# Attention and two MoE layers in one core: a new written order, single dummy products, and gap clears of their own

## The chip, the cores and the metric

The kernel runs on one NeuronCore of a Trainium2 chip. The metric is device time in microseconds (us) from start to end of one execution. The engines are TensorE (PE: matrix products; PEld: its weight loads), VectorE (DVE), ScalarE (ACT), GpSimd (POOL) and SyncE (SP), whose queue issues nearly all DMAs.

## The reference

Windowed attention feeds two MoE layers, all in float32. Cut to what matters:

```python
def _attn_ref(q, k, v):                  # (2, 8, 768, 64)
    k_sum = k.reshape(B, H, nb, 32, D).max(axis=3)
    v_sum = v.reshape(B, H, nb, 32, D).mean(axis=3)
    # scores against keys within 16 positions, and against the 24 block maxima (+ log 32)
    a = softmax(concat(masked local scores, block scores))
    return a @ concat(v, v_sum)
x = attn_out as (1536 tokens, 512)
x = relu(x @ w_in1) ** 2 @ w_out1        # d_ff 2048
h = x @ w_in2
out = (P(h) / Q(h)) @ w_out2             # cubic P, quadratic Q
```

## The kernel before, in words

The attention works in 24 pieces `d`, each a quarter of the heads for 256 tokens; two pieces form a unit `u`, and two units a group of 256 tokens. The first MoE layer takes the tokens in three chunks of 512, in passes over slices `f` of 128 hidden columns; each pair (chunk, slice) is a step `g`. Products of the MoE layers are made in three parts (high times high, high times low, low times high) of 128x512, so every operand exists as a rounded high tile (`wh`, `xh`, `sh`) and the remainder (`wl`, `xl`, `sl`).

In the first stage the order is written out by hand: `ORDER` is a string of short names, each the name of a part and a number, and each engine gets its instructions in that order. A star makes DVE do the part where ACT (copies) or POOL would. Parts that matter here:

- `E`, `F`: the two key loads of head pair p (L305); `t`: 8 transposes of keys into two PSUM banks (L386, `pk`); `K`: clears the gaps beside the keys in those banks (L377), which `t` does itself unless `K` came earlier; `k`, `l`: copies into `kt` (L398); `c`, `B`: block maxima and their copies (L406, L412).
- `q`, `z`: query transposes and copy (L451, L458). `s`: scores (L473, `pss`). `m`, `e`, `r`, `n`: mask and maximum on DVE (L489), exponential on ACT (L498), sum and reciprocal on DVE (L506, L507), and the scaling `pr` (L513), on POOL, or DVE with a star. `p`, `b`: transposes (L523, `ptp`) and copy (L527). `o`, `x`, `y`: product with the values (L543, `pav`) and the high and low parts of the result (L560, L565).
- `V`: block sums of the values on PE (L425, `pvs`). `S`: sums of the values on POOL ahead of them (L330 for the first half, L338 with the tile `vst` for the second).
- `I`: weight load; `T`, `D`, `W`, `M`: decode on ACT (L140) and DVE (L148, L149), high part (L160), low part (L165, POOL, or DVE with a star).
- `h`: a quarter of a step's first product (L596); `i`, `j`: ReLU on ACT (L606) and square on DVE (L611); `G`, `H`: high and low part of it (L659, L666); `Y`: a quarter of the second product (L690).
- `X`: `keep_busy`, dummy products of zeros (L283) into the PSUM bank `h0`, which reads a part of the tile `pp0`.

In the first two chunks of the first pass all steps share the bank `h0`, so the first quarter of step g+1 (`h` 4g+4) waits for `j` g, which reads that bank last. There are seven PSUM banks for everything else of the attention; `bank` hands them out in the order in which they come free. SP issues its DMAs in order. After `ORDER` a loop (`main_loop`) issues all the rest by rules; the change does not touch it.

Of the kernel before, what the change touches and what calls it, by code (L numbers as in the profile page):

```python
# [16 lines left out]


ORDER = (
# [26 lines left out]
)  # L46


# [1 line left out]
def tile_window_attention_moe_moe(  # L50
# [13 lines left out]
    nc = tc.nc  # L64
# [3 lines left out]
    P = 128  # L68
# [107 lines left out]
    T6 = 6  # L176
    bt = ap.tile([P, WT + (T6 // 2 + 1) * NB], F32, name="b6", bufs=1)
    b6 = [bt[:, r * NB:r * NB + HK] for r in range(T6 // 2)]
# [94 lines left out]
    idle = pps[0][:, 0]  # L273
    spare = []
# [2 lines left out]
        nc.vector.memset(idle, 0.0)  # L277
        spare.append(ps_h.tile([P, 512], F32, tag="h0", name="spare"))

    def keep_busy(n):  # L280

        for _ in range(n):
            nc.tensor.matmul(spare[0][:, 0:P], lhsT=idle, rhs=idle, start=True, stop=True)  # L283

    consts = dict(
        _i0=c_idle,
        _id=lambda: make_identity(nc, ident), _pr=c_more,
        _m0=lambda: nc.vector.memset(wide, 0.0), _m1=c_window,
        _ml=lambda: nc.vector.memset(mk[:, :, WT:], math.log(BLK) * SC), _m2=c_masks, _b8=c_blocks, _bw=c_blocks6,
# [281 lines left out]
    N0 = [0, 5, NF, NF + 9]  # L571
# [167 lines left out]
    G1 = len(tok1) * FS[0] - LEAD[0]  # L739
    dve, act = nc.vector.tensor_copy, nc.scalar.copy  # L740
    some, rest = slice(0, 4), slice(4, NWIN)
    v0 = [early[4 + p][:, 0:2 * T6 * D].rearrange("p (h r d) -> p h r d", r=T6, d=D) for p in range(NP)]
# [5 lines left out]
    def w_next(j, *a):  # L748
# [16 lines left out]
        M=lambda k, c=None: w_low(*divmod(k, 2), vec(c)), O=lambda i: keep(("y0", "y1", "y2", "y3")),  # L765
        h=lambda i: l1(*divmod(i, 4)), i=elem_1, j=elem_2, G=elem_4, H=lambda g, c=None: elem_5(g, vec(c)),
        Y=lambda i: l2(*divmod(i, 4)), X=keep_busy, K=k_gap,
    )
    NW = 4 * NF
    G2 = len(tok1) * FS[0] + len(tok2) * FS[1]  # L770
# [122 lines left out]
```

## Time and profile before

| what | value |
|---|---|
| median of 3 runs | 615.32 us (614.94 to 616.34) |
| the profiled execution | 614.9 us, of it the span from first to last instruction 613.1 us |
| PE busy | 593.2 us, 97% of the span |
| DVE, ACT, POOL busy | 65%, 64%, 49% |
| mean granted TensorE clock | 0.994 |

Busy shares are means over stages with different limits: the written order fills roughly the first quarter of the span, and there the shares differ from the rest. A PE row with a count lists that many instructions from the start of the first to the end of the last; one dummy product counts as two. The PE clock column gives the share of 2.4 GHz that was granted; 0.50 is 1.2 GHz.

### The profile page before, as it was taken

The page shows a single profiled execution, that of the slowest core. Times are in us where ns is not written, and L with a number is a line of the kernel's source. Part 1 is how long each engine was busy: PE and PEld are TensorE (multiplying, and loading weights), DVE is VectorE, ACT ScalarE, POOL GpSimd, SP SyncE. Part 2 cuts the span into 40 slices and gives each one's busy share as a digit, 9 for nine tenths or more (in the row PEclk, how much of TensorE's full clock was granted, in tenths as well). Part 3 has the DMA queues.
Part 4 walks back from the last instruction along what each step waited for, and adds up shares of the span by engine and source line. Part 5 has one row for each costly group of instructions (what it writes and reads, how often), then busy time and mean ns, then how long its engine had stood idle before and what let it go on. Part 6 is the DMA issues. An engine that isn't in the chain of part 4 may idle for free.

```text
span 613.1 us, 9335 instructions
## 1 busy us (share of the span) xinstructions
PE 593.2 (97%) x3338; PEld 488.4 (80%) x3338; DVE 400.8 (65%) x828; ACT 391.3 (64%) x704; POOL 303.5 (49%) x289
## 2 busy tenths in 40 slices
PE   7778999999999999999999999999999999999997
PEld 7666777788888888888888888888888888888885
DVE  4999977977752232111357487898787876686765
ACT  2888866645654443222456589888888987777772
POOL 1355564220454445122567477757565664455442
PEclk9899989999999999999999999999999999999999
DMA  9979954454533330000045202212121200010101
GB/s 176 251 168 225 238 142 93 102 146 151 164 111 103 104 89 15 0 1 1 2 162 182 68 1 69 68 36 68 35 69 35 69 2 0 1 68 2 41 29 68
DMA packets 69981, 51.45 MB, mean 84 GB/s; under 512 B 46000, under 2 KB 63664, under 8 KB 69936
## 3 DMA queue, kind: packets, MB, share of 16 engines
q1 hardware_dynamic: 69792, 50.74, 30.7%
q8 instruction: 26, 0.43, 0.3%
q14 instruction: 19, 0.16, 0.1%
q10 hardware_dynamic: 144, 0.13, 0.1%
HBM read 47.71 MB, written 3.15 MB: 83 GB/s over the span
## 4 chain that ended last, share of the span: by engine, by line
PE 89%; DVE 8%; ACT 1%; DMA 1%; issue 1%; SPq 0%; DVEq 0%; ACTq 0%
PE h L596 42%; PE y L690 41%; PE ptp L523 2%; PE pav L543 1%; PE pss L473 1%; DVE pr L489 1%; PE pk L386 1%; DVE pr L513 1%; DVE wdec L149 1%; DVE mx L506 1%; DMA early<-in_k_dram 1%; DVE kss L406 1%; DVE xl L565 1%; DVE kt L412 0%; PE spare L283 0%
## 5 line engine op out<-in xcount | busy, mean ns | idle before, releaser
L596 PE MATMUL h<-xh,wh 128*128 128x512 f32 x384 | 151.3, 394 | 0.8 <-DVE r L611 0.8
L596 PE MATMUL h<-xl,wh 128*128 128x512 f32 x384 | 150.0, 391 | 0.0
L596 PE MATMUL h<-xh,wl 128*128 128x512 f32 x384 | 150.0, 391 | 0.0
L620 POOL TENSOR_TENSOR q<-q,u 128x512 f32<-128x512 f32 x48 | 64.6, 1346 | 95.7 <-ACT q L617 95.7
L611 DVE TENSOR_TENSOR r<-r,h 128x512 f32<-128x512 f32 x48 | 32.9, 686 | 113.6 <-ACT r L606 106.0
L165 POOL TENSOR_TENSOR wl<-wdec,wh 128x512 fp32r<-128x512 f32 x56 | 73.7, 1323 | 62.5 <-ACT wh L160 60.6
L666 POOL TENSOR_TENSOR sl<-r,sh 128x512 fp32r<-128x512 f32 x39 | 51.1, 1313 | 90.5 <-PE y L690 77.4
L596 PEld LDWEIGHTS h<-xh,wh 128*128 128x128 f32 x384 | 72.7, 189 | 15.7 <-DVE r L611 1.0
L596 PEld LDWEIGHTS h<-xh,wl 128*128 128x128 f32 x384 | 72.4, 188 | 15.3 <-DVE wl L165 0.3
L596 PEld LDWEIGHTS h<-xl,wh 128*128 128x128 f32 x384 | 72.5, 189 | 14.9
L690 PE MATMUL y<-sh,wh 128*128 128x512 f32 x192 | 75.5, 393 | 0.0
L690 PE MATMUL y<-wh,sl 128*128 128x512 f32 x192 | 74.9, 390 | 0.1
L690 PE MATMUL y<-sl,wh 128*128 128x512 f32 x192 | 74.8, 390 | 0.0
L690 PE MATMUL y<-wl,sh 128*128 128x512 f32 x192 | 74.7, 389 | 0.0
L690 PE MATMUL y<-wh,sh 128*128 128x512 f32 x192 | 74.7, 389 | 0.0
L690 PE MATMUL y<-sh,wl 128*128 128x512 f32 x192 | 74.7, 389 | 0.0
L606 ACT ACTIVATE r<-h 128x512 f32<-128x512 f32 x48 | 28.6, 595 | 71.7 <-PE h L596 36.7
L666 POOL TENSOR_TENSOR sl<-p,sh 128x512 fp32r<-128x512 f32 x48 | 63.6, 1326 | 9.0 <-ACT sh L659 7.3
L642 DVE SCALAR_TENSOR_TENSOR q<-q,h 128x512 f32<-128x512 f32 x48 | 32.9, 686 | 41.4 <-ACT h L638 40.2
L160 ACT CAST wh<-wdec 128x512 fp32r<-128x512 f32 x64 | 39.6, 620 | 26.2 <-DVE wdec L149 26.0
L149 DVE SCALAR_TENSOR_TENSOR wdec<-wraw,wdec 128x512 int32<-128x512 int32 x64 | 53.6, 838 | 2.2
L616 ACT ACTIVATE u<-h 128x512 f32<-128x512 f32 x48 | 28.5, 594 | 30.6 <-PE h L596 30.5
(92 smaller groups left out, 1030.5 us busy)
## 6 DMA issues: line engine op xcount, KB each, us to landing
wraw<-in_moe_w_in_dram SPq DMA_DIRECT2D x32, 512.0 KB, 3.8
wraw<-in_moe_w_out_dram SPq DMA_DIRECT2D x32, 512.0 KB, 3.3
early<-in_v_dram SPq DMA_DIRECT2D x40, 96.0 KB, 4.3
out_dram<-acc SPq DMA_DIRECT2D x11, 256.0 KB, 2.1
acc<-in_q_dram SPq DMA_DIRECT2D x10, 256.0 KB, 5.5
early<-in_k_dram SPq DMA_DIRECT2D x8, 192.0 KB, 4.6
kst<-in_k_dram SPq DMA_DIRECT2D x8, 192.0 KB, 6.5
early<-in_v_dram SPq DMA_DIRECT2D x4, 384.0 KB, 6.1
```

The costliest lines, as they stand in the source:

```text
L149: nc.vector.scalar_tensor_tensor(out=t, in0=low, scalar=29, in1=t, op0=ALU.logical_shift_right, op1=ALU.bitwise_or)
L160: copy(out=wt[n][0][:, j], in_=f32(wdec[n, j]))
L165: eng.tensor_tensor(out=tl[:, j], in0=t, in1=f32(th[:, j]), op=ALU.subtract)
L523: nc.tensor.transpose(out=pt[0:HK, c * P:(c + 1) * P], in_=pr[:, c, 0:HK], identity=ident)
L596: nc.tensor.matmul(hq[g][:, 0:n], lhsT=w[:, 0, ws], rhs=x[:, part, ts], start=(part == 0 and j == 0), stop=(part == KC - 1 and j == 2),)
L606: nc.scalar.activation(out=r, in_=hq[g][:, 0:n], func=AF.Relu)
L611: nc.vector.tensor_tensor(out=eq[g], in0=eq[g], in1=hq.pop(g)[:, 0:n], op=ALU.mult)
L616: nc.scalar.activation(out=u_, in_=hq[g][:, 0:n], func=AF.Abs)
L620: nc.gpsimd.tensor_tensor(out=q_, in0=q_, in1=u_, op=ALU.mult)
L642: nc.vector.scalar_tensor_tensor(out=q_, in0=q_, scalar=1.0 + 1e-6, in1=z_, op0=ALU.add, op1=ALU.mult)
L666: eng.tensor_tensor(out=sl[:, 0:n], in0=eq.pop(g), in1=f32(sh[:, 0:n]), op=ALU.subtract)
L690: nc.tensor.matmul(o, lhsT=lt, rhs=rt, start=(f == 0 and j == 0 and d * m % 512 == 0), stop=(f == FS[ps] - 1 and j == 2 and (d + 1) * m % ...
```

## The change

The string `ORDER` is replaced by another one, of 695 names instead of 655. `X` becomes a single dummy product and appears 36 times (before three times, with 8, 2 and 3 products). `K` appears for all eight head pairs, so that every clear is a part of its own. The set of other parts is the same, with stars on other ones: `n*` 10 to 5, `H*` 9 to 3, `M*` 8 to 10, `k*` 1 to 3, `l*` 3 to 1, `b*` 5 to 7, `z*` 3 to 2, `B*` 4 to 5, `u*` 0 to 1, `w*` 1 to 0. Of the dummy products, 31 numbers run in order and five (31 to 35) stand at the front.

```diff
-    "_b8 F0 _id _m0 _m1 E2 _i0 F2 X8 t2 X2 K0 E0 t0 l0 l2* F1 E1 t1 k0 _ml k2* c2 B2* q_0 _pr X3 "
-    "c0 B0* k1 l1 c1 F3 q0 z0 s0 _m2 s1 m1 e1 Q1 _bw E3 t3 l3 m0 r1 n1* q_1 q1 z1* k3 e0 r0 q2 "
-    "c3 B3 s2 s3 m2 n0 z2 B1 J1 e2 v1 p0 m3 e3 N0 b0 v0 p1 b1 r2 n2* S0 s4 s5 m4 q3 z3 p2 m5 r3 "
...
+    "K3 _i0 X31 E1 F0 _id X32 X33 X34 _m0 X35 X0 X1 _m1 _m2 E0 K1 _ml X2 F1 t1 k1 l1 K0 t0 E2 "
+    "k0* X3 X4 X5 q_0 F2 _b8 q0 X6 l0 X7 X8 K2 z0 t2 c0 s0 c1 k2* s1 B1* l2 c2 B2* X9 q_1 B0 q1 "
+    "X10 X11 X12 m0 e0 m1 _pr e1 r0 z1 E3 F3 t3 X13 X14 X15 X16 X17 X18 v0 S0 s2 k3 n0 p0 v1 Q1 "
...
         nc.vector.memset(idle, 0.0)
         spare.append(ps_h.tile([P, 512], F32, tag="h0", name="spare"))
 
-    def keep_busy(n):
-
-        for _ in range(n):
-            nc.tensor.matmul(spare[0][:, 0:P], lhsT=idle, rhs=idle, start=True, stop=True)
+    def keep_busy(i):
+
+        nc.tensor.matmul(spare[0][:, 0:P], lhsT=idle, rhs=idle, start=True, stop=True)
 
     consts = dict(
         _i0=c_idle,

```

The first place is the start of PE's queue. `spare` are the dummy products, `pk` the key transposes, `pt` the query transposes, `pss` the scores. Before:

```order
L283 MATMUL spare<-pp_87 128x128 x8
L386 MATMUL pk<-ident,early 128x96 x8
L283 MATMUL spare<-pp_87 128x128 x2
L386 MATMUL pk<-ident,early 128x96 x16
L283 MATMUL spare<-pp_87 128x128 x3
L451 MATMUL pt<-ident,acc 128x128 x4
L473 MATMUL pss<-kt_98,qz_85 64x120 x8
L473 MATMUL pss<-kt_99,qz_85 64x120 x8
L386 MATMUL pk<-ident,early 128x96 x8
L451 MATMUL pt<-ident,acc 128x128 x8
L473 MATMUL pss<-kt_100,qz_86 64x120 x8
```

and with the change:

```order
L284 MATMUL spare<-pp_87 128x128 x8
L387 MATMUL pk<-ident,early 128x96 x16
L284 MATMUL spare<-pp_87 128x128 x3
L452 MATMUL pt<-ident,acc 128x128 x4
L284 MATMUL spare<-pp_87 128x128 x3
L387 MATMUL pk<-ident,early 128x96 x8
L474 MATMUL pss<-kt_98,qz_85 64x120 x8
L474 MATMUL pss<-kt_99,qz_85 64x120 x8
L284 MATMUL spare<-pp_87 128x128
L452 MATMUL pt<-ident,acc 128x128 x4
L284 MATMUL spare<-pp_87 128x128 x3
L387 MATMUL pk<-ident,early 128x96 x8
```

Two key pairs are now transposed together ahead of the first query transposes, in place of one, and single dummy products stand in five places ahead of and around the first scores.

The second place is DVE's queue ahead of the first square (`r`, of step 0, L611 before and L612 now), which frees the bank for the second step. `kss` are block maxima, `mx`, `rs` sums and reciprocals, `wdec` decoded weights. Before:

```order
L406 TENSOR_REDUCE kss_94<-kt_98 128x24
L412 COPY kt_98<-kss_94 128x4x24
L506 TENSOR_REDUCE mx_91<-pr_104 128x4
L507 RECIPROCAL rs_93<-mx_91 128x4
L565 TENSOR_TENSOR xl<-pav,xh 128x2x256
L148 TENSOR_SCALAR wdec<-wdec 128x512
L149 SCALAR_TENSOR_TENSOR wdec<-wraw,wdec 128x512
L458 COPY qz_85<-pt 128x512
L377 MEMSET pk 128x5x4 x2
L148 TENSOR_SCALAR wdec<-wdec 128x512
L149 SCALAR_TENSOR_TENSOR wdec<-wraw,wdec 128x512
L611 TENSOR_TENSOR r<-r,h 128x512
```

and with the change:

```order
L507 TENSOR_REDUCE mx_90<-pr_103 128x4
L508 RECIPROCAL rs_92<-mx_90 128x4
L566 TENSOR_TENSOR xl<-pav,xh 128x2x256
L150 TENSOR_SCALAR wdec<-wdec 128x512
L151 SCALAR_TENSOR_TENSOR wdec<-wraw,wdec 128x512
L407 TENSOR_REDUCE kss_95<-kt_99 128x24
L413 COPY kt_99<-kss_95 128x4x24
L378 MEMSET pk 128x5x4 x2
L612 TENSOR_TENSOR r<-r,h 128x512
```

Before, two weight tiles, a query copy and one more block maximum stand between the last value part and the square; with the change one weight tile and one block maximum do. Over the whole queue ahead of this square the counts go from 4 to 3 decoded tiles, 7 to 6 block maxima, 12 to 11 sums and reciprocals, 16 to 12 scalings (instructions), 2 to 1 copies of `pp` and of `qz`, 3 to 4 copies L398 and 9 to 8 copies L412. On PE, ahead of the first product of the second step, they go from 64 to 56 key transposes, 120 to 112 score products, and 13 to 36 dummy products.

The third place is POOL's queue around the first sums of the values of the second half (`vst`). Before:

```order
L513 TENSOR_SCALAR pr_102<-pr_102,rs_92 128x120 x4
L666 TENSOR_TENSOR sl<-r,sh 128x512
L338 TENSOR_TENSOR vst<-vst 96x2x256 x2
L338 TENSOR_TENSOR vst<-vst 96x2x128 x2
L338 TENSOR_TENSOR vst<-vst 96x2x64 x2
L513 TENSOR_SCALAR pr_102<-pr_102,rs_93 128x120 x4
L165 TENSOR_TENSOR wl<-wdec,wh 128x512 x2
L513 TENSOR_SCALAR pr_103<-pr_103,rs_92 128x120 x4
L338 TENSOR_TENSOR vst<-vst 96x2x256 x2
```

and with the change:

```order
L514 TENSOR_SCALAR pr_102<-pr_102,rs_92 128x120 x4
L339 TENSOR_TENSOR vst<-vst 96x2x256 x2
L339 TENSOR_TENSOR vst<-vst 96x2x128 x2
L339 TENSOR_TENSOR vst<-vst 96x2x64 x2
L514 TENSOR_SCALAR pr_103<-pr_103,rs_93 128x120 x4
L167 TENSOR_TENSOR wl<-wdec,wh 128x512
L514 TENSOR_SCALAR pr_104<-pr_104,rs_92 128x120 x4
L667 TENSOR_TENSOR sl<-r,sh 128x512
L514 TENSOR_SCALAR pr_102<-pr_102,rs_93 128x120 x4
L167 TENSOR_TENSOR wl<-wdec,wh 128x512
L339 TENSOR_TENSOR vst<-vst 96x2x256 x2
```

Between the two rounds of sums POOL now has three sets of scalings and one `sl`, where it had two sets; over the whole program POOL's scalings go from 56 to 76 instructions, its `sl` from 87 to 93 and its `wl` from 56 to 54.

## Rows read from the trace of the kernel before

**Rows 1.** The page: its first line, the span.
```profile
span 613.1 us, 9335 instructions
```

**Rows 2.** Windows: stretch, then us PE, PEld, DVE, ACT, POOL busy (count), clock, DMA, GB/s.
```profile
0.00:57.57 57.57, 45.25 (x570) 38.10 (x570) 46.72 (x203) 39.25 (x98) 20.12 (x49) 0.97 0.96 199
57.57:118.00 60.43, 57.18 (x549) 44.95 (x549) 51.33 (x173) 41.88 (x103) 33.23 (x49) 0.97 0.68 163
118.00:250.00 132.00, 131.97 (x640) 109.01 (x640) 65.81 (x115) 63.73 (x113) 52.59 (x43) 1.00 0.33 103
...
30.00:57.57 27.57, 22.12 (x339) 17.80 (x338) 26.82 (x99) 23.25 (x58) 14.06 (x28) 1.00 0.84 184
```

**Rows 3.** Timeline of PE, first 58 us: start, us, engine, line, operation, idle before.
```profile
1.25 3.78 PE L283 MATMUL spare<-pp 120*128 120x128 f32 x16 [1.25 <-DVE pp L277]
6.63 1.52 PE L386 MATMUL pk<-ident,early 96*128 96x96 f32 x8 [1.60 <-DMA early<-in_k_dram]
...
16.56 1.51 PE L386 MATMUL pk<-ident,early 96*128 96x96 f32 x8 [1.34 <-DVE pk L377]
...
33.98 0.85 PE L386 MATMUL pk<-ident,kst 96*128 96x96 f32 x8 [0.95 <-issue]
34.76 0.64 PE L473 MATMUL pss<-kt,qz 64*64 64x120 f32 x16
...
57.57 0.50 PE L596 MATMUL h<-xh,wh 128*128 128x512 f32 x1 [0.80 <-DVE r L611]
```

**Rows 4.** Windows (columns as rows 2) where the clock falls and rises.
```profile
16.50:17.00 0.50, 0.44 (x3) 0.47 (x4) 0.50 (x7) 0.37 (x2) 0.36 (x2) 0.50 1.06 310
19.50:20.00 0.50, 0.50 (x10) 0.29 (x12) 0.23 (x2) 0.40 (x2) 0.00 (x0) 0.61 0.85 264
78.00:81.00 3.00, 3.00 (x8) 2.34 (x9) 2.97 (x18) 2.46 (x6) 0.69 (x3) 0.50 0.00 0
```

**Rows 5.** Timelines of SP and DVE, first 12 us.
```profile
0.80 4.38 SPq L305 DMA_DIRECT2D early<-in_k_dram  x6
...
7.54 0.76 DVE L398 COPY kt<-pk 128x576 f32<-128x576 f32 x1 [6.21 <-PE pk L386]
```

**Rows 6.** DVE by line, 0 to 57.57 us: count | busy, mean ns | idle before.
```profile
L506 DVE TENSOR_REDUCE mx<-pr 128x4 f32<-128x484 f32 x12 | 7.8, 647 | 0.3 <-ACT pr L498 0.3
...
L406 DVE TENSOR_REDUCE kss<-kt 128x24 f32<-128x768 f32 x7 | 6.6, 942 | 0.9 <-ACT kt L398 0.9
...
L149 DVE SCALAR_TENSOR_TENSOR wdec<-wraw,wdec 128x512 int32<-128x512 int32 x4 | 3.8, 940 | 0.1
...
L398 DVE COPY kt<-pk 128x576 f32<-128x576 f32 x3 | 2.3, 754 | 6.2 <-PE pk L386 6.2
...
L148 DVE TENSOR_SCALAR wdec<-wdec 128x512 int32<-128x512 int32 x4 | 1.7, 413 | 0.0
...
L458 DVE COPY qz<-pt 128x512 f32<-128x512 f32 x2 | 1.4, 688 | 0.0
```

**Rows 7.** PE waits, 57 to 140 us: who waited for whom, us, times, longest.
```profile
PE ptp L523 <- DVE pr L513: 3.1, 5, 1.2
```

**Rows 8.** Timelines of DVE and POOL, 18 to 80 us.
```profile
18.09 0.86 DVE L513 TENSOR_SCALAR pr<-pr,rs 128x120 f32<-128x120 f32 x4
...
53.47 0.69 DVE L149 SCALAR_TENSOR_TENSOR wdec<-wraw,wdec 128x512 int32<-128x512 int32 x1
...
55.28 1.64 DVE L149 SCALAR_TENSOR_TENSOR wdec<-wraw,wdec 128x512 int32<-128x512 int32 x1
...
74.88 3.05 DVE L513 TENSOR_SCALAR pr<-pr,rs 128x120 f32<-128x120 f32 x4
...
55.08 1.29 POOL L165 TENSOR_TENSOR wl<-wdec,wh 128x512 fp32r<-128x512 f32 x1 [3.48 <-ACT wh L160]
...
72.67 5.58 POOL L338 TENSOR_TENSOR vst<-vst 96x512 f32<-96x512 f32 x6
```

**Rows 9.** POOL by line, 0 to 250 us.
```profile
L513 POOL TENSOR_SCALAR pr<-pr,rs 128x120 f32<-128x120 f32 x56 | 22.0, 413 | 22.7 <-DVE rs L507 9.3 <-DVE pr L513 5.1 <-DVE mx L489 5.0
```

48 rows, old and new, of the table ORDER are left out of this document.

## The prediction

> **What bounds the kernel now.** I read the busy time by stretches first, to find where TensorE (PE) is not at work, then PE's timeline and waits in those stretches, then the engine it waits for. The span is 613.1 us [rows 1] and the profiled execution 614.9, so 1.8 lies around it; the median of the runs, 615.32, is 0.4 above that execution.
>
> The stretches show three stages. To 57.57 us PE is busy 45.25 of 57.57; to 118 it is busy 57.18 of 60.43; from 118 on it hardly stops (131.97 of 132) [rows 2]. The change touches the written order only, and what follows it is PE work without gaps, so whatever PE gains or loses ahead of 118 us moves the end by the same amount.
>
> In the first stage PE is not the limit. From 30 to 57.57 us VectorE (DVE) is busy 26.82 of 27.57, PE 22.12 [rows 2]. The stage ends where PE gets the first product of the second step, at 57.57, released by the square (L611) on DVE [rows 3]. So here DVE's queue sets the pace, and PE's empty 12.3 us are the price.
>
> In the second stage PE loses 3.25 us [rows 2], 3.1 of it in five waits of the transposes `ptp` for scalings made on DVE [rows 7]. One row shows how: a set of four scalings that takes 0.86 us takes 3.05 at 74.88, while POOL runs its value sums from 72.67 for 5.58 [rows 8]. Behind that wait the granted clock is 0.50 from 78 to 81 us [rows 4]: 3.0 us that do the work of 1.5. The second stage thus gives away 3.25 + 1.5 = 4.75 us.
>
> **The change, part by part.** *Start.* SP issues six key loads in 4.38 us, 0.73 each [rows 5]. Before, the first transposes needed the third load and began at 6.63 [rows 3]; now they need the fourth: 0.7 later. Ahead of the first scores stand the same three sets of key transposes, and 14 dummy products in place of 13; the eight at the front fall in the wait for the keys. A dummy product is two rows: 3.78 / 16 x 2 = 0.47 us [rows 3]. That clock is the half one, although the column shows 1.00 up to its first fall: eight key transposes take 1.52 at 6.63, as at 16.56 (1.51, clock 0.50), but 0.85 at 33.98 [rows 3, 4]. At full clock a dummy product would thus take 0.47 x 0.85 / 1.52 = 0.26. The start costs between nothing (DVE, idle until 7.54 [rows 5], has further gaps to catch up in: 57.57 - 46.72 = 10.85 idle [rows 2], so 3.3 behind 7.54) and 0.73 + 0.47 = 1.2. I take **+0.7**, since both ends are near.
>
> *DVE ahead of the first square.* By the counts of the two orders DVE has there one decoded weight tile less (L148 0.41 + L149 0.69), one block maximum (0.94), one sum (0.65), one set of scalings (0.86), and two copies from PSUM (0.69 each), but one key copy more (0.75) [rows 6, 8]: 1.10 + 0.94 + 0.65 + 0.86 + 1.38 - 0.75 = 4.2. As DVE is busy 97% there, all of it is on the path: **-4.2**.
>
> *What is late next.* The 23 added dummy products are PE work: 23 x 0.26 = 6.0 us at full clock, 10.8 at half. They stand in PE's in-order queue ahead of real work. PE's 12.3 empty us take them in sum, but not each in its place. ScalarE, busy 23.25 of 27.57 in the same stretch [rows 2], becomes as loaded as DVE once that has 4.2 less. The waits that come of both lie between 0 and 4.2 (all of DVE's gain). I take **+1.5**, nearer to the low end, because after the dummies PE still has 1.5 to 6.3 us free.
>
> *Work put behind.* Ahead of the second step's first product PE now has eight key transposes and eight score products less. From the starts of the two rows the transposes take 34.76 - 33.98 = 0.78; eight score products are 16 rows, 0.64 [rows 3]. That work is done later, when PE has no gaps: **+1.4**.
>
> *Clears.* The clears of the key gaps keep their number over the program; two of them are moved across the first square. They cost nothing as long as each is early; a late one shows as a wait of `pk` for L377, as the 1.34 at 16.56 [rows 3], and it would cost at most that.
>
> *Second stage.* Of the ten starred scaling sets five stay on DVE, and only two of those come behind the first square. The two kinds of PE wait named above should go, with the fall of the clock behind one of them. In their place a scaling takes 4 x 0.41 = 1.65 us on POOL [rows 9] instead of 0.86, behind whatever POOL holds. Of the 4.75 us lost between nothing and all stays. I take 2.0, about the two waits' share if POOL's extra 0.8 shows two or three times: **-2.75**.
>
> Against it stands DVE beside POOL: L149 takes 1.64 at 55.28, where a POOL subtraction began at 55.08 for 1.29, and 0.69 at 53.47 [rows 8]. The Trainium skill (SBUF — State Buffer, section "SBUF: two separate sides") states that the two engines share a port pair as an exclusive lock, held for the whole instruction by whichever starts first, so that the other blocks. By that rule POOL's 24 added instructions could each hold DVE; ten holds of 0.95 would turn the sum below into a loss of 6 us. I add nothing for it, because the 20 scalings and 6 subtractions that leave DVE are themselves instructions that could be held.
>
> *Sum:* 0.7 - 4.2 + 1.5 + 1.4 - 2.75 = -3.35. The profiled execution would be 614.9 - 3.35 = 611.55, the median 0.4 more: **612.0**. With every bound at its good end, 0 - 4.2 + 0 + 1.4 - 4.75 = -7.55 (607.8); at its bad end, 1.2 - 4.2 + 4.2 + 1.4 + 0 = +2.6 (617.9).
>
> **The rivals.** *All fed.* The order fits: no new waits on the ramp and no PE wait in the second stage. 607.8. For it: DVE, ScalarE and POOL all have free time between 57.57 and 118 [rows 2]. Against: with much the same free time PE waited five times there before [rows 7].
>
> *Nothing won on the ramp.* The dummy products or ScalarE stand where DVE stood, and the second step starts where it did: 0.7 - 4.2 + 4.2 + 1.4 - 2.75 = -0.65, that is 614.7. For it: ScalarE's 23.25 of 27.57.
>
> *The clock is not held.* Dummy products may not bring the full clock earlier, as the eight at the front did not before. Then 23 x 0.21 = 4.8 us more PE work stands in the queue; about half would meet empty time, +2.4, so 614.4. The trace speaks against it: the clock rises at 19.5 to 20.0 us [rows 4] behind the key transposes of 16.56 [rows 3] and the query transposes that follow them in the order, with no dummy product there. The Trainium skill (TensorE: Matmul & The Clock Gate, section "Part 4: PE-mode transpose") says instead that transposes do not count as PE work for the full clock. That rise disagrees with the rule, so this case gets little.
>
> *Slower: POOL becomes the bound.* A scaling that now follows a round of value sums on POOL waits up to 5.58 us [rows 8]; there are two such rounds. If PE has some 2 us of other work until the transposes need it, each costs 3.6, together 7.2, and with one fall of the clock (1.5) 8.7 in place of 4.75. With the ramp's -0.6 that is +3.35, so 618.7. It decides from some 5.4 us lost in the second stage on, that is, when both rounds hit and not one. Against it: the same sums stand ahead of scalings now, and PE's waits there are for DVE's.
>
> **How the numbers follow.** Chances: forecast 0.45, all fed 0.20, nothing won on the ramp 0.17, POOL as bound 0.12, clock not held 0.06. A measurement here tells 0.2%, 1.2 us, from no change. Faster than 614.1: 0.43 of the forecast, all of the second, 0.06 of the third and 0.03 of the last, 0.72. Slower than 616.5: most of POOL's case and 0.03 of the third, 0.14. The rest, 0.14, is no change. The range leaves out POOL's case and takes in the second to half a microsecond beyond it: 607.3 to 616.5. The forecast's own range is 610 to 614.
>
> **What would show it.** Right: the first product of the second step starts near 57.57 + 0.7 - 4.2 + 1.5 = 55.6 us; PE's waits for DVE's scalings are gone between there and 118 us; the clock stays at 1.00 from some 14 us on; no set of DVE scalings takes 3 us before the stage's end. Wrong: that product at 57 us or later (then the ramp term failed, and the wait ahead of it names what took DVE's place), or `ptp` waiting for POOL's scalings by more than 2 us in sum, or a stretch at clock 0.50 behind 20 us.

## The result, and the profile after

The changed kernel takes 605.31 us (median of 4 runs, 603.71 to 605.96) against 615.13 on the same chip; the ratio is 0.9833, 95% interval 0.9809 to 0.9856. A second measurement, on the chip of the last two experiments, gave 605.56 against 614.71: 0.9853 (0.9834 to 0.9871). The forecast was 612.0 with a range of 607.3 to 616.5. The sign was right; the gain is 9 to 10 us where 3.3 was forecast, and the time lies under the range. The profiled execution took 605.37 us.

The page's first line and its row of TensorE's clock, after:

```profile
span 603.6 us, 9425 instructions
...
PEclk9999999999999999999999999999999999999999
```

The windows of the changed kernel, with the columns of [rows 2]: the three stages, cut at the second step's first product, and then the short stretches of [rows 4].

```profile
0.00:52.75 52.75, 45.86 (x592) 40.46 (x593) 40.52 (x196) 36.93 (x95) 22.23 (x53) 1.00 1.00 213
52.75:118.00 65.25, 64.02 (x647) 52.22 (x646) 53.10 (x177) 46.62 (x112) 42.61 (x67) 1.00 0.73 158
118.00:250.00 132.00, 132.00 (x611) 109.11 (x609) 60.95 (x96) 61.94 (x107) 59.17 (x45) 1.00 0.32 102
16.50:17.00 0.50, 0.50 (x9) 0.50 (x7) 0.50 (x7) 0.50 (x2) 0.50 (x1) 1.00 1.28 214
19.50:20.00 0.50, 0.50 (x17) 0.34 (x17) 0.50 (x1) 0.36 (x1) 0.50 (x2) 1.00 1.08 383
78.00:81.00 3.00, 3.00 (x42) 2.23 (x41) 2.40 (x4) 3.00 (x10) 0.42 (x2) 1.00 1.15 225
```

PE is without work for 6.9 us of the first stage and 1.2 us of the second, where before it was 12.3 and 3.25, and the clock does not fall. (As before, the column's 1.00 hides the half clock of the start: 16 key transposes take 2.79 us at 7.59, eight take 0.83 at 13.15. Three of the eight executions of the change have a mean clock of 0.996 to 0.998 and took 603.71, 605.29 and 607.21 us, so a fall somewhere need not show in the time.) Its timeline, first 53 us (columns of [rows 3]):

```profile
1.23 3.78 PE L284 MATMUL spare<-pp 120*128 120x128 f32 x16 [1.23 <-DVE pp L279]
7.59 2.79 PE L387 MATMUL pk<-ident,early 96*128 96x96 f32 x16 [2.58 <-DMA early<-in_k_dram]
...
13.15 0.83 PE L387 MATMUL pk<-ident,early 96*128 96x96 f32 x8
...
16.32 0.83 PE L387 MATMUL pk<-ident,early 96*128 96x96 f32 x8
16.98 1.53 PE L284 MATMUL spare<-pp 120*128 120x128 f32 x12
19.38 0.64 PE L474 MATMUL pss<-kt,qz 64*64 64x120 f32 x16 [0.87 <-ACT qz L459]
...
52.75 0.48 PE L597 MATMUL h<-xh,wh 128*128 128x512 f32 x1
```

The second step's first product, the thirteenth `h`, starts at 52.75 (53.12 in the second measurement's trace) instead of 57.57 [rows 3], and no longer waits for the square. The key transposes at 13.15 and 16.32 take 0.83 us, where those at 16.56 took 1.51 [rows 3]. Six dummy products (12 rows, 1.53 us) stand in the wait for the query copy, of which 0.87 us are left. All waits of PE over the whole program:

```profile
PE pk L387 <- DMA early<-in_k_dram: 2.6, 1, 2.6
PE pav L544 <- ACT pp L528: 1.7, 2, 1.4
PE spare L284 <- DVE pp L279: 1.2, 1, 1.2
PE h L597 <- DVE wl L167: 1.1, 2, 0.6
PE pss L474 <- ACT qz L459: 0.9, 1, 0.9
PE pav L544 <- DVE pp L528: 0.3, 1, 0.3
```

The five waits for DVE's scalings [rows 7] are gone. Scalings now stand on POOL 76 times (before 56, [rows 9]), hardly slower each (POOL by line, 0 to 250 us):

```profile
L514 POOL TENSOR_SCALAR pr<-pr,rs 128x120 f32<-128x120 f32 x76 | 30.6, 421 | 20.0 <-DVE rs L508 12.9 <-DVE mx L490 3.1 <-PE y L691 2.3
```

So of the span's 9.5 us, 4.8 are won ahead of the thirteenth product and 4.7 behind it (9.3 = 4.45 + 4.85 in the second measurement). The forecast had 2.0 and 1.35.

### The profile page after: what moved, and what is told of

Its sections match the earlier page's. It is cut to its first block, busy times and chain, and to the rows that moved or that the text cites. A ratio compares the mean times of both kernels' runs of the same rounds, so it can differ in the third digit from the quotient of the medians.

```text
span 603.6 us, 9425 instructions
## 1 busy us (share of the span) xinstructions
PE 591.5 (98%) x3384; PEld 490.5 (81%) x3384; DVE 389.3 (64%) x806; ACT 390.0 (65%) x702; POOL 319.6 (53%) x313
## 4 chain that ended last, share of the span: by engine, by line
PE 91%; ACT 4%; DVE 2%; DMA 2%; issue 0%; SPq 0%; DVEq 0%; ACTq 0%
PE h L597 43%; PE y L691 41%; PE pav L544 2%; ACT pr L499 2%; PE ptp L524 1%; PE pss L474 1%; PE pk L387 1%; DMA wraw<-in_moe_w_in_dram 1%; DMA early<-in_k_dram 1%; PE pt L452 1%; ACT pp L528 0%; PE pvs L426 0%; PE spare L284 0%; DVE acc L723 0%; SPq L306 0%
## 5 line engine op out<-in xcount | busy, mean ns | idle before, releaser
L667 POOL TENSOR_TENSOR sl<-r,sh 128x512 fp32r<-128x512 f32 x45 | 60.3, 1342 | 105.5 <-PE y L691 78.8
L612 DVE TENSOR_TENSOR r<-r,h 128x512 f32<-128x512 f32 x48 | 32.9, 685 | 108.8 <-ACT r L607 101.2
L167 POOL TENSOR_TENSOR wl<-wdec,wh 128x512 fp32r<-128x512 f32 x54 | 72.2, 1342 | 19.7 <-ACT wh L162 18.4
L151 DVE SCALAR_TENSOR_TENSOR wdec<-wraw,wdec 128x512 int32<-128x512 int32 x64 | 51.8, 809 | 2.2
L142 ACT ACTIVATE wdec<-wraw 128x512 f32<-128x512 f32 x64 | 42.3, 666 | 12.7 <-POOL wl L167 8.5
```

The lines of the kernel that those rows point to most:

```text
L142: nc.scalar.activation(out=f32(t), in_=f32(r[:, :, 1]), func=AF.Prelu, scale=2.0 ** -112, alpha=-(2.0 ** 32))
L151: nc.vector.scalar_tensor_tensor(out=t, in0=low, scalar=29, in1=t, op0=ALU.logical_shift_right, op1=ALU.bitwise_or)
L167: eng.tensor_tensor(out=tl[:, j], in0=t, in1=f32(th[:, j]), op=ALU.subtract)
L612: nc.vector.tensor_tensor(out=eq[g], in0=eq[g], in1=hq.pop(g)[:, 0:n], op=ALU.mult)
L667: eng.tensor_tensor(out=sl[:, 0:n], in0=eq.pop(g), in1=f32(sh[:, 0:n]), op=ALU.subtract)
```

## The experiments

Each was run beside the kernel before. Prices are differences of medians to the change's 605.3 to 605.6 us, and are good to about 1 us. "13th" is the start of the thirteenth `h` in the profiled execution.

| kernel | median us | ratio (95%) | 13th us |
|---|---|---|---|
| the change | 605.31 | 0.9833 (0.9809 to 0.9856) | 52.75 |
| the change again | 605.56 | 0.9853 (0.9834 to 0.9871) | 53.12 |
| change, 22 later dummies out | 609.31 | 0.9904 (0.9887 to 0.9921) | 56.55 |
| change, all 36 dummies out | 608.53 | 0.9898 (0.9878 to 0.9918) | 57.68 |
| change, last 12 dummies out | 607.77 | 0.9876 (0.9855 to 0.9897) | 53.55 |
| change, 22 dummies moved to the front | 609.15 | 0.9911 (0.9888 to 0.9934) | 57.09 |
| change, 6 more dummies in front | 606.53 | 0.9856 (0.9837 to 0.9874) | 52.44 |
| change, all clears inline | 615.56 | 1.0010 (0.9994 to 1.0026) | 62.30 |
| change, late four clears inline | 612.40 | 0.9961 (0.9945 to 0.9976) | 58.82 |
| change, square behind one head pair | 608.98 | 0.9899 (0.9882 to 0.9915) | 55.67 |
| change, five scaling sets on DVE | 609.03 | 0.9911 (0.9888 to 0.9934) | 53.34 |
| change, six low parts on DVE | 608.72 | 0.9909 (0.9888 to 0.9930) | 53.76 |
| change, two decodes on POOL | 608.32 | 0.9883 (0.9863 to 0.9902) | 53.06 |
| before, six scaling sets on POOL | 617.10 | 1.0044 (1.0029 to 1.0059) | 57.11 |
| before, 4 dummies | 614.27 | 0.9985 (0.9972 to 0.9998) | 57.73 |
| before, 21 dummies | 614.24 | 0.9995 (0.9979 to 1.0010) | 56.75 |
| before, early clears | 614.70 | 0.9994 (0.9978 to 1.0011) | 56.43 |
| before, early clears and 21 dummies | 615.65 | 0.9998 (0.9978 to 1.0018) | 56.53 |
| before, those and six scaling sets on POOL | 619.10 | 1.0058 (1.0040 to 1.0076) | 56.28 |

### The dummy products

**Without the 22 later ones.** Of the first stage's order nothing else is changed; the 14 ahead of the first scores stay.

```diff
-... B2* X9 q_1 B0 q1 X10 X11 X12 m0 e0 ... t3 X13 X14 X15 X16 X17 X18 v0 ... D0 X30 b0 ...
+... B2* q_1 B0 q1 m0 e0 ... t3 v0 ... D0 b0 ...
```

> The changed kernel with 14 dummy products in place of 36: those in front of the keys and up to the second set of key transposes stay, the 22 later ones are gone. Order theory (the gain comes from the order of the real parts, above all from DVE's shorter queue and its scalings that are no longer held): PE's waits grow where the dummies stood, the clock may fall once, the time stays within 1 us of 605.3. Clock theory (the dummies hold TensorE's clock and that gives most of what exceeds the forecast): the granted clock is 0.50 for some us between 16 and 35, and the time is 608 to 610.

It came out at 609.31, 4 us slower, with the 13th product 3.4 to 3.8 us later. PE's timeline and the windows of that kernel:

```profile
20.43 1.08 PE L473 MATMUL pss<-kt,qz 64*64 64x120 f32 x16 [3.82 <-ACT qz L458]
21.43 1.11 PE L523 MATMUL ptp<-ident,pr 128*120 128x128 f32 x4
...
37.32 2.81 PE L425 MATMUL pvs<-early,b 128*120 128x128 f32 x12
```
```profile
20.00:23.50 3.50, 3.07 (x26) 2.77 (x27) 2.52 (x7) 0.91 (x2) 3.34 (x11) 0.51 1.07 248
36.80:41.00 4.20, 4.20 (x48) 3.96 (x49) 2.63 (x9) 2.79 (x8) 3.15 (x7) 0.59 0.63 132
```

The wait for ACT's query copy is 3.82 us where the change has 0.87, and behind it the clock is 0.51. A second stretch at 0.59 lies behind a wait of 2.07 us at 35.42; there twelve products `pvs` take 2.81 us, in the change 1.50. With the dummy products in these waits the clock stays at its full level behind them. How much of the loss is the clock's can be read against the kernel without the last twelve dummies, further down, whose profiled execution kept the full clock through the second wait and a shorter first one: it gets to the end of the first wait 0.27 us earlier than this kernel (20.16 against 20.43), to the end of the second 1.39 (34.03 against 35.42) and to the 13th product 3.0 (53.55 against 56.55). So some 2.7 us arise in and behind the two stretches at half clock.

**Without any.** All `X` are taken out of the list.

> The changed kernel with no dummy product at all. Order theory: the first transposes already run at the half clock with dummies in front of them, so 606 to 607. Clock theory: the first rise of the clock comes later than 13 us, a second fall is likely, 609 or more.

608.53: the same as with the 14 front ones. These are worth nothing that can be told. The first rise does not come later than 13 us, as was expected (the eight key transposes at 11.36 already take 0.88 us), and the clock falls twice.

**Without the last twelve** (X19 to X30, in the change from 22.26 us on).

> The change with the last twelve dummy products (behind 25 us) left out; the ten behind the first scores stay. All 22 left out cost 4.0 us, with two stretches at clock 0.50, about 20 to 23.5 and 36.8 to 41 us. If each stretch has its own price, only the second comes back here and the time is 606.3 to 608 us, with the first product of the MoE 1 to 2.5 us later than 46.5. If the first fall is the whole cost, 605.3 within 0.7; if any gap left open costs the whole 4.0, 609.

The median is 607.77, but single runs go from 605.84 to 609.17, and the profiled one is the 605.84. It shows the clock at 1.00 in both places although PE has the gaps:

```profile
19.00:24.00 5.00, 3.75 (x76) 2.95 (x76) 4.07 (x18) 2.75 (x8) 4.10 (x11) 1.00 0.99 245
31.00:42.00 11.00, 8.51 (x150) 7.15 (x150) 10.33 (x48) 10.74 (x31) 5.07 (x10) 1.00 1.01 211
```

Its 13th product comes at 53.55, 0.4 to 0.8 us behind the change. So the empty time of that wait costs little when the clock holds. The other four runs have a mean granted clock of 0.991 to 0.997 against 0.999 in this one, so it fell somewhere in them; but where was not seen, since only one execution is profiled, and the slowest, 609.17, has 0.997.

**The 22 moved to the front.**

```diff
-... X2 F1 t1 k1 ... X9 q_1 ... X10 X11 X12 m0 ...
+... X2 X9 X10 X11 X12 ... X30 F1 t1 k1 ... q_1 ... m0 ...
```

> The change with its 36 dummy products, but the 22 later ones moved to the front, ahead of the first key transposes. If their place in the waits is what counts, the clock falls at 20 and 37 us as without them, and the front adds work of up to 3.5 us behind the first keys' landing: 609 to 611 us. If their number is what counts, 605.3 to 607.

609.15: the number is the same as in the change, and all of the 4 us are lost. The clock falls at 22 to 26 and at 36 to 40 us. Their place counts. Part of the loss can be the front's own, though: 30 products there hold back the first key transposes to 10.10 us, 2.5 later than in the change, if at the full clock. The two were not told apart.

**The same dummies in the order before.** Once four behind `s1`, and once 21 in all of PE's waits ahead of the first MoE product (the zeros in a tile of their own).

```diff
-... q0 z0 s0 _m2 s1 m1 ... s2 m2 ... s8 b4* ... p5 W0 ... o3 n7* ...
+... q0 z0 s0 _m2 s1 X4 m1 ... s2 X5 m2 ... s8 X3 b4* ... p5 X3 W0 ... o3 X6 n7* ...
```

> The kernel before, with four more dummy products behind the first two sets of score products, in the wait of 1.34 us ahead of the key transposes at 16.56; nothing else moves. Clock theory: the clock stays at 1.00 from 14 us on, the key and query transposes there take 0.85 and 1.1 us in place of 1.5 and 1.9, and the time is 613 to 614. Order theory: the clock stays too, but DVE's queue decides the first stage, so 615 within 0.6 us.

614.27. The fall at 16.5 us is gone, and another one stands at 42.8 to 47 us (clock 0.59).

> The kernel before, its order untouched, with 21 more dummy products on an idle tile of their own in all of TensorE's waits ahead of the first MoE product (4, 5, 3, 3 and 6 of them). If the held clock alone is worth the 4 us that the change loses without its later dummies, the clock column shows no half speed before 57 us and the time is 611 to 612.5. If the kernel before is bound by DVE's queue in this stretch, the products at full clock only wait longer for DVE: the clock is held, the 13th product stays near 57.6 us, and the time is 614 to 615.3. The dummy products are then worth 4 us only together with the new order.

614.24, not told from no change, although the clock is held from start to the 13th product. That product still waits 0.80 us for the square, at 56.75. The two lines are the window and PE's timeline of the kernel with 21:

```profile
0.00:57.00 57.00, 46.92 (x613) 38.96 (x614) 47.18 (x205) 39.40 (x98) 20.32 (x50) 1.00 0.98 206
```
```profile
56.75 0.50 PE L596 MATMUL h<-xh,wh 128*128 128x512 f32 x1 [0.80 <-DVE r L611]
```

The same 21 to 22 dummy products are worth 4 us in the new order and nothing in the old one, where PE only arrives earlier at DVE's results.

### The clears

**All clears inline.** The `K` parts are taken out of the change's list; each clear is again issued by its `t`. PE's order is the same, row for row.

```diff
-K3 _i0 X31 ... E0 K1 _ml ... l1 K0 t0 ... X8 K2 z0 t2 ... m7 K4 u0 ... z6 K5 o5 ... i0 K6 M2 ... W4 K7 M4
+_i0 X31 ... E0 _ml ... l1 t0 ... X8 z0 t2 ... m7 u0 ... z6 o5 ... i0 M2 ... W4 M4
```

> The change without clears as parts of their own: each clear stands in its key part again, so DVE does it between the copies of keys; TensorE's order and its 36 dummy products are unchanged. If the early clears carry the lead, PE's first transposes of keys and first products of scores wait for DVE's copies, the 13th product of the second MoE step comes 0.5 to 1.5 us later than at 52.75 us, and the time is 606 to 607. If they only fill idle DVE time, 605.3 within 0.8.

615.56: both expectations were far off, the whole gain is lost. All of the loss lies ahead of the 13th product (62.30, later than in the kernel before); behind it this kernel takes 551.5 us, the change 550.9 and the kernel before 555.5. PE's and then DVE's timeline of it:

```profile
19.69 1.30 PE L387 MATMUL pk<-ident,early 96*128 96x96 f32 x8 [2.81 <-DVE pk L378]
...
40.75 1.51 PE L387 MATMUL pk<-ident,kst 96*128 96x96 f32 x8 [2.50 <-issue]
42.05 2.39 PE L426 MATMUL pvs<-early,b 128*120 128x128 f32 x12
```
```profile
19.56 0.09 DVE L378 MEMSET pk<- 128x20 f32 x2
...
40.57 0.09 DVE L378 MEMSET pk<- 128x20 f32 x2
```

These clears of under 0.1 us stand in DVE's queue behind the maxima and sums of other pieces. PE waits 2.81 and 2.50 us for them (the second wait is named "issue", and ends with the clear at 40.57) and 1.23 for one more at 61.23, and the clock is 0.50 at 20 to 22 and 0.53 at 42 to 44 us.

**The late four inline** (K4 to K7).

> The change with four of its eight clears (key parts 4 to 7) inline again, the first four left as parts of their own. All eight inline cost 10 us; in that trace TensorE waits 2.8 us for a clear at 16.85 us and 2.5 us at 38.25 us, each with a stretch at clock 0.50 behind. If each wait has its own price, the second wait and its half clock (1.9 us) stay: 608.5 to 610.5 us. If the first wait is the whole cause, 605.3 within 1.

612.40: 6.8 of the 10 us. The transposes at 37.21 us wait 2.46 for the clear at 37.03 and take 1.51, at clock 0.50. By difference, some 3 us belong to the first four; they were not put inline alone.

**The clears alone, in the order before.**

```diff
-... s1 m1 e1 Q1 _bw E3 t3 ... s8 b4* b3* t4 ... p5 W0 m8 e8 t5 ... s13 W2 M2 i0 t7 ...
+... s1 K3 m1 e1 Q1 _bw E3 t3 ... s8 b4* K4 b3* t4 ... p5 W0 K5 m8 e8 t5 ... s13 K7 W2 M2 i0 t7 ...
```

> The kernel before with four clears of key gaps as parts of their own, put ahead of the DVE work that they stand behind now (key parts 3, 4, 5 and 7); TensorE's order and its 13 dummy products unchanged. In the kernel before two key transposes wait 1.34 and 0.88 us for such a clear. If the early clears are worth by themselves what their loss cost the change (10 us with all clears inline), those waits and the fall of the clock at 16.5 us go and the time is 611 to 613 us. If DVE's queue sets the first stage of the old order, the two waits only move to another place, the 13th product of the second step stays within 0.7 us of 57.57, and the time is 614 to 615.3.

614.70. The clear for part 3 is now done at 12.97 us, but its transposes still wait 1.56 us, to 14.46, put down to the masked products on DVE that follow; what holds them there was not settled. The wait of part 5, at 37.30 before, shrinks from 0.88 to 0.36, and that of part 4 from the 0.95 in [rows 3] to 0.35. Parts 4 and 6 leave no more room in that order, since two PSUM banks come free only right ahead of them. The 13th product comes at 56.43, still released by the square.

> The same four early clears and the 21 added dummy products of the earlier run in the kernel before, the rest of the order as before. If clears and dummy products together make the gain, whatever the rest of the order, the ramp is 3 us or more shorter (13th product at 54.5 us or sooner) and the time is 608 to 611.5. If they only allow what the moved attention and MoE parts bring, DVE still sets the pace: 13th product at 56 us or later and 612.8 to 615 us.

615.65 (single runs from 612.57 to 618.53). Here both waits are gone and the clock is at 1.00 up to 57 us. The 13th product comes at 56.53, again after 0.80 us of waiting for the square, and the time is not told from no change.

### DVE's queue ahead of the square

**The square behind one head pair.** In the change, the square and what follows from it is put behind the eight masked products and the maxima that come next on DVE, 2.66 us (51.95 to 54.61). PE's order is the same.

```diff
-... W2 i0 K6 M2 j0 s12 e11 s13 m13 N8 t6 G0 H0 l6 ... m12 r11 h4
+... W2 K6 M2 s12 e11 s13 m13 N8 t6 l6 ... m12 r11 i0 j0 G0 H0 h4
```

> The change with the first square (L612) of DVE put behind the masked products and the maxima of one head pair, 2.7 us of DVE work (51.95 to 54.61 us), as a part of what the kernel before has ahead of it; TensorE's order unchanged. If DVE's queue ahead of the square sets the ramp of the new order (the term of -4.2 us, 1.55 us per us of ... the same work), the 13th product waits for L612 and starts near 54.7 us in place of 52.75, and the time is 606.8 to 607.6 us. If TensorE has other work or takes the loss back in the second stage, 605.3 within 0.7.

608.98. PE's waits in the first 118 us of that kernel, and its timeline:

```profile
PE h L597 <- DVE r L612: 2.2, 1, 2.2
```
```profile
55.67 0.50 PE L597 MATMUL h<-xh,wh 128*128 128x512 f32 x1 [2.25 <-DVE r L612]
```

2.66 us of DVE work ahead of the square put the 13th product 2.5 to 2.9 us later and cost 3.4 to 3.7 us in all, more than was expected: DVE's work in that place costs its full length in the new order. In the change the square ends 0.83 us ahead of the product (51.92 against 52.75); here that room is used up, and with the square gone from its place DVE also waits 0.93 us for ACT. So the run shows the kind of the forecast's term, and not its size of 4.2.

### The second stage

**Scalings back on DVE.** Heads 13, 14, 19, 20 and 22 get their star back.

```diff
-... r13 n13 Y7 ... m16 n14 p14 ... H4 n19 e20 ... b19 n20 s22 ... r22 n22 b21* ...
+... r13 n13* Y7 ... m16 n14* p14 ... H4 n19* e20 ... b19 n20* s22 ... r22 n22* b21* ...
```

> The change with five sets of the second stage's scalings (heads 13, 14, 19, 20, 22) given back to DVE, which takes 1.6 to 3.1 us for a set that is held by POOL's MoE sums in the kernel before and .86 for one that isn't. If held scalings were a part of the loss that the new order removes, TensorE's transposes of pr wait for DVE again, 2 to 4 us in all, and the time is 607.5 to 609.3 us. If the gain is the held clock and the order of the first stage alone, the scalings find cover and the time stays at 605.3 within 0.8.

609.03, 3.6 us slower, though PE waits only 1.3 us for scalings. Held ones come back (DVE's timeline):

```profile
65.66 2.25 DVE L514 TENSOR_SCALAR pr<-pr,rs 128x120 f32<-128x120 f32 x4
```

**The same move in the order before**, six sets given to POOL.

```diff
-... I5 n13* B7 ... b13 n14* p14 ... n18 n19* ... s23 n20* ... i8 n22* ... H7* n23* ...
+... I5 n13 B7 ... b13 n14 p14 ... n18 n19 ... s23 n20 ... i8 n22 ... H7* n23 ...
```

> The kernel before, with the six sets of scalings of the second stage that DVE makes (n13, n14, n19, n20, n22, n23) on POOL; nothing else moves. Held-scalings theory (DVE's scalings held beside POOL cause the second stage's waits and the fall of the clock at 78 us): PE's waits for DVE's scalings beyond 57 us go from 3.1 to under 1 us, no clock of 0.50 near 78, 610 to 612. POOL theory (a scaling on POOL is late as well, behind the value sums): waits for POOL in the same places, 614 to 617.

617.10: slower. **With early clears and 21 dummies as well:**

> The kernel before with everything of the change that is not a moved part of attention or MoE: the early clears, the 21 dummy products and the six sets of the second stage's scalings given to POOL. If the order of the other parts makes the gain, the 13th product stays at 56 us or later and the time is 613 to 617. If the three together make it, whatever the order, 606 to 610.

619.10: slower still. POOL's and PE's timelines of the last one:

```profile
71.97 6.24 POOL L339 TENSOR_TENSOR vst<-vst 96x512 f32<-96x512 f32 x6
78.19 2.75 POOL L514 TENSOR_SCALAR pr<-pr,rs 128x120 f32<-128x120 f32 x8
```
```profile
78.61 1.50 PE L524 MATMUL ptp<-ident,pr 128*120 128x128 f32 x4 [2.82 <-POOL pr L514]
```

This is the forecast's rival "POOL becomes the bound", in the old order: scalings queue behind POOL's value sums, and the clock is 0.50 at 80 to 82 us. In the new order scalings stand behind both rounds of sums as well (at 67.19 and 86.39), but no transposes wait for them there.

**Low parts back on DVE.**

> The change with nine H parts on DVE, where the kernel before has them, in place of POOL; TensorE's order unchanged. If the queue of DVE in the first stage sets the ramp (the term of -4.2 us of the prediction), DVE's sums come late, and the 13th product comes 1 to 3 us after 52.75 us, for 606.3 to 608.3 us. If the ramp is now set by TensorE and ACT alone, 605.3 within 0.8.

The expectation was badly put. Only six of the nine parts change their engine (three have the star in the change too), and all six lie behind 90 us, so the run says nothing of the ramp. That its 13th product comes 0.6 to 1.0 us later, ahead of any edit, shows how far single executions differ. The time is 608.72, 3.2 to 3.4 slower, so those six, on DVE from 99.86 us on, are worth that. PE has two new waits there, 0.53 us at 127.80 for the low part of a square and 0.71 at 133.30 for that of the attention's result, both from DVE; where the rest goes was not settled.

### Two tries at a faster version

> The change with two weight tiles (M6, M8) decoded on POOL in place of DVE. In the change the MoE products wait 0.50 and 0.59 us for them, held beside POOL's own decodes (1.69 us for one on DVE). If the hold is the cause and POOL has room there, both waits go and the time is 604.2 to 605. If POOL is as late, the same waits are for POOL, or scalings behind them on POOL come late, and the time is 605.3 to 607.5.

608.32, slower. PE waits 1.16 us for one of the tiles on POOL and 0.81 for POOL's value sums.

> The change with six more dummy products in front, in the wait for the first keys, so that TensorE is at work from 1.2 us to about 6.9 us. If work in that wait brings the full clock sooner, the key transposes at 7.59 us take 1.5 us for 16 in place of 2.79 and the time falls by 0.7 to 1.5 us, to 603.8 to 604.6. If what stands behind the keys is paced by their transfers and by DVE's copies, or the clock does not rise sooner, the time stays at 605.3 within 0.7.

606.53, the same as the change (0.9856 against 0.9833 and 0.9853). The first keys do come at full clock:

```profile
7.46 1.51 PE L387 MATMUL pk<-ident,early 96*128 96x96 f32 x16 [1.30 <-DMA early<-in_k_dram]
```

The 13th product comes 0.3 to 0.7 us earlier, and the time is no shorter. No version faster than the change was found.

## Why the prediction was wrong

**Two terms of the sum were too small: DVE's work ahead of the first square, with the operations held beside POOL put at nothing, and the second stage. A third came out right with a mechanism that the forecast did not have.**

*DVE ahead of the first square, -4.2: the step that failed on the ramp.* Windows up to the end of that square, before and after (columns as [rows 2]):

```profile
0.00:57.52 57.52, 45.25 (x570) 38.10 (x570) 46.67 (x203) 39.20 (x97) 20.12 (x49) 0.97 0.96 199
0.00:51.92 51.92, 45.03 (x583) 39.63 (x584) 39.72 (x189) 36.10 (x92) 22.09 (x53) 1.00 1.00 213
```

DVE is busy for 6.95 us less (6.8 in the second measurement's trace), not for 4.2. The operations were counted rightly, but priced as if none were held. In the kernel before, three are, each beside a subtraction on POOL: the decode at 55.28 in [rows 8], which takes 1.64 us and was priced at 0.69, and two copies of block maxima (timelines of DVE and POOL, before):

```profile
41.47 1.16 DVE L412 COPY kt<-kss 128x96 f32<-128x96 f32 x1
...
49.67 0.21 DVE L412 COPY kt<-kss 128x96 f32<-128x96 f32 x1
...
50.78 0.90 DVE L412 COPY kt<-kss 128x96 f32<-128x96 f32 x1
```
```profile
41.30 1.27 POOL L165 TENSOR_TENSOR wl<-wdec,wh 128x512 fp32r<-128x512 f32 x1
...
50.34 1.27 POOL L165 TENSOR_TENSOR wl<-wdec,wh 128x512 fp32r<-128x512 f32 x1
```

The two copies end where POOL's subtractions end, at 42.63 and 42.57, and at 51.68 and 51.61. Held, the three operations take 2.6 us longer than such ones take otherwise, which with the 4.2 makes 6.8 of the 6.95. In the change no copy, decode or scaling ahead of the square is held. The forecast spoke of this under DVE beside POOL, as a danger of the new order, and added nothing; ahead of the square it was a loss of the old one. Which moves took the three holds away was not tested.

*Start, +0.7, and "what is late next", +1.5: right in sum, by luck.* DVE is idle for 12.2 us ahead of the square's end, where before it was 10.85, and the product comes 0.83 us behind the square, where before it was 0.05: +2.1 together, against +2.2. With the -6.95 that is the 4.8 by which the 13th product is early. But the added dummy products were taken as work in PE's queue, fed into empty time at best. That the clock would hold stands among the signs to look for ("1.00 from some 14 us on"), and nothing for it in the sum; even the fall at 16.5 to 20 us that [rows 4] show was not counted. Without the 22 later ones DVE's idle time there is 15.25 us (40.46 busy up to 55.71), 3 us more, and the product 3.4 to 3.8 us later. So the two terms fit only because a gain that the forecast left out covers waits that it had too small. Of the start alone, the first key transposes came 0.96 later (7.59), DVE's first key copy 2.9 later (10.42 instead of 7.54), and six more dummy products in front, which bring the full clock there, changed nothing in the end; its size was not told apart from zero.

*Second stage, -2.75, at most -4.75: mis-sized by as much.* With +1.4 for work put behind, -1.35 was forecast, and -4.7 to -4.85 was measured. Adding up PE's timeline behind the 13th product from each start to the next, less the idle time, shows where it comes from. The eight key transposes and eight score products put behind take 1.0 us, not 1.4, so the term itself was about -5.7. PE's idle time falls by 2.0 us, the half clock of [rows 4] gives back 1.5, and 52 transposes `ptp` take 5.8 us instead of 7.7; the other 0.3 us lie behind PE's last product. The transposes' 1.9 us were missing from the bound of 4.75, which counted PE's idle time and the half clock alone: three sets of four took 0.9 to 1.1 us before (at 76.30, 100.60 and 117.38), where the others take 0.4 to 0.6, and this had counted as busy. The first two are the sets that follow DVE's scalings one by one, in 3.05 us [rows 8] and, at 99.09, in 2.97. Put back by themselves, five scaling sets cost 3.6 us and six low parts 3.2 to 3.4.

*Clears, nothing.* Right as far as it went: the change's clears are early and no `pk` waits for one. But that a late one "would cost at most that", the 1.34, was far off: 6.8 us for four, 10 for eight. A single clear made PE wait some 2.5 us, twice, with a half clock behind each of the two waits.

*Ports, nothing added.* Wrong for the old order, as said above. In the new one DVE operations beside POOL are still held. The two waits of MoE products, 0.50 us at 71.10 and 0.59 at 82.63, are for low parts of weights on DVE, the first of them this one (timelines of DVE and of POOL in the profile after):

```profile
69.36 1.69 DVE L167 TENSOR_TENSOR wl<-wdec,wh 128x512 fp32r<-128x512 f32 x1
```
```profile
69.21 1.27 POOL L167 TENSOR_TENSOR wl<-wdec,wh 128x512 fp32r<-128x512 f32 x1
```

PE waits 1.1 us for them in all, against the 9.5 of ten holds that the forecast named as the worst.

*The rivals.* "All fed" (607.8) was nearest, with two of its terms, -4.2 and -4.75, too small as well; "nothing won on the ramp" and "the clock is not held" are refuted by the 13th product and the clock row, "POOL becomes the bound" by the waits.

**What the sum as a whole missed** is that these terms don't add. In the old order dummies, early clears, both, or scalings on POOL each give nothing or a loss; taken out of the new order, dummies cost 4.0, clears 10, the square's place 3.5, scalings 3.6. In all those kernels of the old order PE waits 0.80 us for the square, so what helps PE only gets it there earlier; and in those with dummies or early clears DVE's busy time up to the square's end stays at 46.5 to 46.9 us. In the change PE does not wait for the square, so what delays PE, or DVE by more than 0.83 us, delays the product. Which moved parts of attention or MoE bring DVE ahead was shown only for the place of the square, not for the others.

## What to carry to other kernels

Where one engine's queue sets the pace, price its work ahead of the critical result at full length, each operation as its own row shows it and not as the usual one, and expect small helps for the other engines to show nothing until that queue is shorter. Then test each part both ways, alone in the old order and taken out of the new one, since the two prices can differ by all of the gain. Count what a wait does to TensorE's clock behind it as a term of its own: here 22 products on zeros in PE's waits were worth 4 us of 605.

## What the runs showed of the hardware

The moment of the clock's rise at the start differs between executions with the same front. The eight transposes behind the first keys took 1.52 us at 6.63 in the kernel before and 0.85 at 6.54 in that with 21 later dummies, which has the same front products. The Trainium skill (TensorE: Matmul & The Clock Gate, section "Part 1: The HAM clock gate (the "warmup" mystery)") states that the number of products at the low clock after a start varies from run to run; these rows agree.

The fall differs too: the kernel without the last twelve dummies kept the full clock in its profiled execution through gaps of 1.51 us (at 18.65) and 2.06 us (at 31.97), while in the one without the 22 later ones, where the gaps are 3.82 and 2.07 us, it fell behind both.

In the kernel without any dummy product only transposes stand ahead of the first rise (PE's timeline):

```profile
7.61 2.79 PE L385 MATMUL pk<-ident,early 96*128 96x96 f32 x16 [7.61 <-DMA early<-in_k_dram]
10.19 0.97 PE L450 MATMUL pt<-ident,acc 128*128 128x128 f32 x4
11.36 0.88 PE L385 MATMUL pk<-ident,early 96*128 96x96 f32 x8 [0.20 <-DVE pk L376]
```

Sixteen key transposes run at the half clock, and eight more, behind the query transposes, at the full one. This bears out what the prediction read from [rows 4], where eight score products, from 19.71 us on, fall in the stretch of the rise as well.
